# Row sums of a modulation vector on VectorE, a gate applied out of PSUM, and a bfloat16 exponential in a linear-attention and GEGLU block

## The chip, the cores and the metric

The kernel runs on 1 core of a Trainium2 chip. The metric is the device time of one execution in microseconds (us), as a median of several executions. Engines are named as in the profile: TensorE is PE (its weight loads PEld), VectorE is DVE, ScalarE is ACT, GpSimd is POOL and SyncE is SP. DMAs that an engine issues stand in its own queue, in order.

## The reference, cut to what matters

```python
mod = (silu(c) @ w_mod).reshape(...)          # 6 rows of 1024: sa, ca, ga, sb, cb, gb
h = layernorm(x) * (1 + ca) + sa
q, k, v = h @ wqkv                            # 32 heads of 32
phi = lambda t: where(t > 0, t + 1, exp(t)) + 1e-06
kv = einsum('bhsd,bhse->bhde', phi(k), v);  z = sum over s of phi(k)
o = (phi(q) @ kv) / (phi(q) . z + 1e-06)      # per head
x = x + ga * (o @ wo)
h = layernorm(x) * (1 + cb) + sb
x = x + gb * ((gelu(h @ w_gate) * (h @ w_up)) @ w_down)
```

Inputs are bfloat16: 2048 tokens of 1024 features, w_down has 3584 rows.

## The kernel before, in words

Sequence chunks are 128 tokens (16 of them), four chunks make a sequence group (sg). The work runs in stages along TensorE's queue:

- Start, 0 to 27 us: layer norm of the first chunks, and the modulation columns sa and ca by 128 narrow matmuls (L803).
- Feature-map stage, 27 to 127 us: blocks of 8 matmuls for k (L919) and q (L970), each into one PSUM bank. `phi` (L903) takes a bank out: ScalarE writes exp into a tile EB (L908), VectorE clamps EB in place (min 1, add 1e-6, L909), and VectorE adds max(bank, 0) and writes bfloat16 (L911). EB is float32, 128x512, five buffers.
- m tiles and W2, 127 to 205 us: 24 tiles of 16 matmuls (`m_tile`, L934; numbered 0 to 23 here) form phi(k)^T x per head group g. ScalarE copies a tile out (L939), SyncE issues a transposing DMA (`m_t`, tile mtb), `kv_prod` (L952) multiplies with the v weights, VectorE masks the result into KVT (L956, called kvt0 to kvt7), and `w2_pair` (L1235) multiplies KVT with two halves of wo. ScalarE copies the pair of banks out into W2 (L1237).
- From 192 us `wo_mm` (L1304) multiplies scaled phi(q) with W2, VectorE adds the residual (L1313, L1317), and the second layer norm and the GEGLU part (L1475, L1688) follow.

Four pieces of work are woven into the m tiles. The table `HOOK` in the code says after which tile each is recorded.

1. *The other modulation rows.* For half rows k = 0 to 7 (ga: 0 and 1; sb and cb: 2 to 5; gb: 6 and 7) VectorE accumulates silu(c) times w_mod, 8 steps of 128x512 each (macc, L855 and L858; for gb L833 and L835). The sum over the 128 partitions is done on TensorE: ScalarE rounds an accumulator to bfloat16 (mhi, L864, L842), VectorE takes the remainder (mlo, L868, L843), and `mod_rows` (L879) multiplies both with a column of ones, 8 matmuls of 32 columns by 256 or 512. ScalarE copies the bank (L886) and SyncE stores the row to DRAM (scr_row, L888). It is read back as a broadcast row (gab, L894, the gate ga on all partitions; gbb for gb) or as columns (sbT and cbT, L1252).
2. *The gate.* VectorE multiplies each of the 8 row blocks of wo with gab before W2 is formed (wofold, L1241).
3. *The denominators.* VectorE forms z32 (L1229). `den` (L1262) makes 32 matmuls for two sequence groups into bank 5; VectorE adds 1e-6 (dene, L1267), takes reciprocals (rden, L1268) in the buffer RDC and copies them to bfloat16 in the buffer RDH (rdenh, L1269). There is one RDC and one RDH. A store writes RDH to DRAM (scr_rd, L1271). den0 stands after tile 16 and its store directly behind it; den1 stands after tile 19.
4. *Scaling.* SyncE loads the factors back as broadcasts (rb, L1283) and VectorE scales phi(q) with them (pqs, L1296).

The order on VectorE, ScalarE and GpSimd from 27 us on isn't the recorded one: `Sched.reorder` sorts the operations by due times that it works out from a table of costs (`COST`) and from what depends on each. TensorE and SyncE keep the recorded order. Each engine waits on semaphores in its own order, so an operation that waits holds all behind it on that engine.

Of the kernel before, what the change touches and what calls it, by code (L numbers as in the profile page):

```python
# [7 lines left out]
ACTF = mybir.ActivationFunctionType  # L8
ALU = mybir.AluOpType

P = 128
# [178 lines left out]
class Sched:  # L190
# [41 lines left out]
    def dma(self, stream, fn, rd=(), wr=(), deps=(), note="", overwrite_ok=False):  # L232
# [6 lines left out]
        if prev is not None:  # L239
# [12 lines left out]
               "nm": (0.074, 0.085), "hmod": (0.25, 0.085), "macc": (0.66, 0.085), "mlo": (0.6, 0.085), "kvt": (0.21, 0.085), "z": (0.34, 0.085),  # L252
               "dene": (0.335, 0.085), "rden": (1.67, 0.085), "pqs": (0.62, 0.085), "wofold": (1.13, 0.085), "x": (1.14, 0.085), "ssum": (1.15, 0.085), "tsum": (1.15, 0.085), "padd": (0.62, 0.085), "yT": (0.62, 0.085)},
# [96 lines left out]
def bass_adaLN_cond__linear_attn_block__geglu_ffn__prompt_kernel(  # L350
# [18 lines left out]
    with ExitStack() as es:  # L369
# [48 lines left out]
        EB = [at(f"eb{i}", [P, 512], f32, EBO[i]) for i in range(5)]  # L418
# [4 lines left out]
        MROW = [at(f"mrow{i}", [P, 512], f32, OFF_ROW + i * 2048) for i in range(2)]  # L423
        MROW0 = at("mrowa", [P, 256], f32, XHO[2])
        WMG = [at(f"wmg{i}", [P, 4, 512], bf16, HBO[3] + i * 4096) for i in range(2)]
        MRG = at("mrg", [P, 256], f32, OFF_TMP + 4096)
        HLG = at("hlg", [P, 2, 2, 512], bf16, OFF_TMP)
        GAC = at("gacc", [P, 512], f32, OFF_TMP + 4096)
        ACC = [at(f"acc{i}", [P, 512], f32, OFF_ROW + i * 2048) for i in range(2)]
        HLO = OFF_WS + 16384  # L430
        HL = at("hl", [P, 4, 2, 512], bf16, HLO)
# [7 lines left out]
        for name, shape, dty, sz in [  # L439
            ("ident", [P, P], bf16, 256), ("bmask", [P, P], bf16, 256), ("bm32", [P, NG, NH], bf16, 512),   # L440
            ("z32", [P, NG, NH], bf16, 512), ("rdc", [P, SGW // 2], f32, 1024), ("rdh", [P, SGW // 2], bf16, 512),
            ("ones", [P, 32], bf16, 64), ("silf", [P, NDC], f32, 64),
# [14 lines left out]
        ONES, SILF, C8, CT, CHALF, THC, SILUT = (_small[k] for k in ("ones", "silf", "c8", "cT", "chalf", "thc", "siluT"))  # L457
# [78 lines left out]

        def r_hl(k, h0, h1):
            return [(HLO + (2 * (k % 4) + h0) * 1024, HLO + (2 * (k % 4) + h1) * 1024, "hl")]
# [131 lines left out]
        sch.op(V, lambda e: e.memset(ONES[:, :], 1.0), wr=r_sm("ones"))  # L670
# [155 lines left out]
        def r_hlg(j, h):  # L826
            return [(OFF_TMP + (2 * j + h) * 1024, OFF_TMP + (2 * j + h + 1) * 1024, "hlg")]

# [11 lines left out]
        def gb_hilo(j):  # L840
            acc, rng = GA_[j]
            sch.op(A, lambda e: e.activation(HLG[:, j, 0, :], acc[:, :], ACTF.Copy), rd=rng, wr=r_hlg(j, 0), note=f"mhi{6 + j}")  # L842
            sch.op(V, lambda e: e.tensor_tensor(HLG[:, j, 1, :], acc[:, :], HLG[:, j, 0, :], ALU.subtract), rd=rng + r_hlg(j, 0), wr=r_hlg(j, 1), note=f"mlo{6 + j}")  # L843

        o_gb = [None]

        def gb_rows():
            mod_rows(((0, 2, 5, lambda j, h: (HLG[:, j, h, :], r_hlg(j, h))),))
            o_gb[0] = mod_store(2, 5, MRG, [(OFF_TMP + 4096, OFF_TMP + 5120, "mrg")], 2)
# [12 lines left out]
        def mod_hi(k):  # L862
            rng = r_2k(OFF_ROW + k % 2 * 2048, f"acc{k % 2}")
            sch.op(A, lambda e: e.activation(HL[:, k % 4, 0, :], ACC[k % 2][:, :], ACTF.Copy), rd=rng, wr=r_hl(k, 0, 1), note=f"mhi{k}")  # L864

        def mod_lo(k):
            rng = r_2k(OFF_ROW + k % 2 * 2048, f"acc{k % 2}")
            sch.op(V, lambda e: e.tensor_tensor(HL[:, k % 4, 1, :], ACC[k % 2][:, :], HL[:, k % 4, 0, :], ALU.subtract),  # L868
                   rd=rng + r_hl(k, 0, 1), wr=r_hl(k, 1, 2), note=f"mlo{k}")

        def mod_rows(parts):
            for k0, n, bank, src in parts:
                o = None
                w = n * P
                for h in range(2):
                    for j in range(4):
                        ap, rng = src(k0 + j * n // 4, h)
                        ap = ap[:, j * w % 512:j * w % 512 + w]
                        o = sch.op(T, lambda e, h=h, j=j, ap=ap, bank=bank, w=w: e.matmul(  # L879
                            ps_all[32 * j:32 * (j + 1), bank * 512:bank * 512 + w], ONES[:, :], ap, start=(h == 0), stop=(h == 1)),  # L880
                            rd=rng + r_sm("ones"), pwr=(pr(bank) if h == j == 0 else ()), note=f"modr{k0}.{h}.{j}")
                pset_writer(bank, o)

        def mod_store(n, bank, dst, rng, row):
            w = n * P
            sch.op(A, lambda e: e.activation(dst[:, 0:w], ps_all[:, bank * 512:bank * 512 + w], ACTF.Copy),  # L886
                   prd=pr(bank), wr=rng, note=f"mrow{row}")
            return sch.dma(Q, lambda e: e.dma_start(scr_row[row, 0:n, :].rearrange("a (h b) -> (a h) b", b=w), dst[0:128:32, 0:w]), rd=rng, note=f"mrow{row}.st")  # L888

        def hl_src(k, h):  # L890
            return HL[:, k % 4, h, :], r_hl(k, h, h + 1)
# [214 lines left out]

        def wofold(*kcs):
            for kc in kcs:
                rg = r_wo(kc)
                sch.op(V, lambda e, kc=kc: e.tensor_tensor(WO[:, kc, :], WO[:, kc, :], GAB[:, :], ALU.mult),  # L1110
                       rd=rg + R_GAB, wr=rg, note=f"wofold {kc}")
# [978 lines left out]
```

## Time and profile before

| | |
|---|---|
| median of 3 runs | 784.59 us (783.88 to 785.09) |
| the profiled execution | 784.2 us, its span 782.4 us |
| TensorE's granted clock | 1.000 |
| VectorE, ScalarE busy in the span | 83%, 45% |
| 0 to 27 us, TensorE busy | 22.85 us |
| 27 to 127 us, TensorE / VectorE / ScalarE busy | 99.47 / 91.89 / 70.04 us |
| 127 to 205 us, TensorE / VectorE / ScalarE busy | 77.53 / 56.17 / 24.61 us |
| 205 to 260 us, TensorE / VectorE busy | 54.64 / 46.74 us |
| 260 to 600 us, TensorE / VectorE busy | 338.18 / 298.47 us |
| 600 to 782.4 us, TensorE / VectorE busy | 178.88 / 138.16 us |

The span goes from the first to the last instruction; the time of an execution is 1.8 us longer. A duration of one instruction in the groups includes its fill, so that the next one can start before it ends; where two follow each other, the distance of their starts is the cost. Line numbers are those of the kernel before; in the changed kernel the functions from `phi` on stand 27 to 41 lines higher.

### The profile page before, as it was taken

To read this page: it belongs to the slowest core of one execution; us is meant where nothing else is said; L and a number is where in the kernel's file an instruction comes from. 1 tells how busy PE (TensorE), PEld (TensorE's weight loads), DVE (VectorE), ACT (ScalarE), POOL (GpSimd) and SP (SyncE) were. 2 spreads that over 40 slices of the span, in tenths; PEclk is the share of its full clock that TensorE was granted. 3 is DMA by queue.
4 is the path that set the end of the run, shared out by engine and by line. 5 is a ranking of instruction groups with operands and counts; after the bars stand their busy time and mean duration, and the time that the engine had idled before them with its cause. 6 is when DMAs were issued, how large, how long until landed. Compare 5 with 4: busy or idle time off the path is not lost.

```text
span 782.4 us, 11038 instructions
## 1 busy us (share of the span) xinstructions
PE 771.6 (99%) x3812; PEld 501.1 (64%) x3875; DVE 646.0 (83%) x1089; ACT 353.0 (45%) x585; POOL 47.4 (6%) x126
## 2 busy tenths in 40 slices
PE   8999999999999999999999999999999999999998
PEld 4444445666445677767676777767676576677766
DVE  6699989993498978897999989898889897676777
ACT  2497743333474576776554444444544111111111
POOL 2031300000230011110000000000000000000000
PEclk9999999999999999999999999999999999999999
DMA  9889749836597068747445465646545445344341
GB/s 277 261 168 251 156 96 253 222 70 115 133 257 189 28 188 255 210 127 182 125 125 162 135 197 194 194 118 199 148 121 149 155 129 160 121 142 130 120 134 41
DMA packets 210543, 125.93 MB, mean 161 GB/s; under 512 B 70444, under 2 KB 200116, under 8 KB 210488
## 3 DMA queue, kind: packets, MB, share of 16 engines
q1 hardware_dynamic: 210328, 125.16, 58.4%
q8 instruction: 31, 0.51, 0.3%
q14 instruction: 24, 0.20, 0.1%
q10 hardware_dynamic: 160, 0.07, 0.0%
HBM read 88.35 MB, written 23.22 MB: 143 GB/s over the span
## 4 chain that ended last, share of the span: by engine, by line
PE 94%; DMA 2%; SPq 2%; issue 1%; DVE 0%; ACT 0%; DVEq 0%
PE ps_all L1475 45%; PE ps_all L1688 23%; PE ps_all L970 7%; PE ps_all L1304 7%; PE ps_all L934 6%; PE ps_all L919 6%; DMA mtb<-mb 1%; SPq L632 1%; DMA wmq<-in_w_mod_dram 1%; SPq L637 1%; PE ps_all L952 0%; PE ps_all L1235 0%; PE ps_all L1262 0%; SPq L626 0%; DVE xall L1317 0%
## 5 line engine op out<-in xcount | busy, mean ns | idle before, releaser
L1475 PE MATMUL ps_all<-ss,tp 128*128 128x512 f32 x896 | 214.7, 396 | 0.0
L1475 PEld LDWEIGHTS ps_all<-ss,tp 128*128 128x128 f32 x896 | 168.1, 188 | 38.2 <-DVE ps_all L1487 0.6
L1688 PE MATMUL ps_all<-bt,xs 128*128 128x512 f32 (+1 forms) x532 | 125.6, 393 | 0.1
L1688 PEld LDWEIGHTS ps_all<-bt,xs 128*128 128x128 f32 x532 | 98.9, 188 | 22.6 <-issue 0.5
L1487 DVE TENSOR_TENSOR ps_all<-ps_all,es 128x512 f32<-128x512 f32 x112 | 77.6, 696 | 38.4 <-PE ps_all L1475 35.8
L1492 ACT ACTIVATE ge<-ps_all 128x512 f32<-128x512 f32 x112 | 64.0, 597 | 89.1 <-DVE ps_all L1487 45.0
L1496 DVE TENSOR_TENSOR yr<-ge,ps_all 128x512 bf16<-128x512 f32 x112 | 74.0, 679 | 2.2 <-PE ps_all L1475 1.6
L1443 DVE TENSOR_TENSOR tp<-wt 128x512 fp32r<-128x512 bf16 x112 | 74.1, 683 | 1.1 <-DMA wt<-in_B_w_gate_dram 0.7
L1443 DVE TENSOR_TENSOR tp<-wt,tp 128x512 fp32r<-128x512 bf16 x112 | 74.0, 682 | 0.0
L970 PE MATMUL ps_all<-h1T,wq 128*128 128x512 bf16 x256 | 56.7, 379 | 0.0
L919 PE MATMUL ps_all<-wk,h1T 128*128 128x512 bf16 x239 | 55.3, 379 | 1.1 <-DMA wk<-in_A_wqkv_dram 0.5
L1304 PE MATMUL ps_all<-w,pq 128*128 128x512 bf16 x251 | 55.9, 379 | 0.4
L1688 PE MATMUL ps_all<-bx,yl 128*128 128x512 bf16 x225 | 55.2, 380 | 0.7
L1475 PE MATMUL ps_all<-ar,tp 128*128 128x512 f32 x224 | 55.3, 389 | 0.0
L908 ACT ACTIVATE eb<-ps_all 128x512 f32<-128x512 f32 x64 | 36.4, 593 | 37.5 <-PE ps_all L919 15.5
L1475 PE MATMUL ps_all<-h20a,wt 128*128 128x512 bf16 x210 | 48.0, 379 | 0.9
L1475 PE MATMUL ps_all<-h21a,wt 128*128 128x512 bf16 x210 | 47.8, 379 | 1.0
L1475 PEld LDWEIGHTS ps_all<-ar,tp 128*128 128x128 f32 x224 | 42.0, 188 | 8.7
L1484 ACT ACTIVATE es<-ps_all 128x512 f32<-128x512 f32 x56 | 33.4, 599 | 30.8 <-PE ps_all L1475 30.8
L1481 ACT ACTIVATE ps_all<-ps_all 128x512 f32<-128x512 f32 x56 | 32.6, 582 | 31.2 <-PE ps_all L1475 30.9
L970 PEld LDWEIGHTS ps_all<-h1T,wq 128*128 128x128 bf16 x256 | 25.0, 98 | 29.9
L1304 PEld LDWEIGHTS ps_all<-w,pq 128*128 128x128 bf16 x256 | 24.7, 98 | 30.3 <-issue 0.5
(152 smaller groups left out, 889.9 us busy)
## 6 DMA issues: line engine op xcount, KB each, us to landing
wt<-in_B_w_gate_dram SPq DMA_DIRECT2D x28, 512.0 KB, 4.0
wt<-in_B_w_up_dram SPq DMA_DIRECT2D x28, 512.0 KB, 5.4
scr_y<-yr SPq DMA_DIRECT2D x56, 256.0 KB, 4.8
yl<-scr_y SPq DMA_DIRECT2D x8, 896.0 KB, 4.7
yl<-scr_y SPq DMA_DIRECT2D x14, 448.0 KB, 4.4
wmst<-in_w_mod_dram SPq DMA_DIRECT2D x6, 1024.0 KB, 5.5
wmq<-in_w_mod_dram SPq DMA_DIRECT2D x8, 512.0 KB, 6.0
rb<-scr_rd SPq DMA_DIRECT2D x32, 128.0 KB, 2.9
```

Of the source, the lines that this page charges most:

```text
L908: sch.op(A, lambda e: e.activation(EB[i][:, :], PS(bank), ACTF.Exp), prd=pr(bank), wr=rng, note=f"{note}.exp")
L919: o = sch.op(T, lambda e, dc=dc: e.matmul(PS(bank), H1[sg][:, ci, dc, :], W_[:, dc, jg * 512:(jg + 1) * 512], start=(dc == 0), stop=(dc == ...
L934: o = sch.op(T, lambda e, c_=c_: e.matmul(PS(bank, 0, n), PK[c_][:, g * P:(g + 1) * P], xrow(c_, o_, o_ + n), start=(c_ == 0), stop=(c_ == ...
L970: o = sch.op(T, lambda e, dc=dc: e.matmul(PS(b), WQ[:, dc, qc * P:(qc + 1) * P], H1[sg][:, :, dc, :], start=(dc == 0), stop=(dc == NDC - 1 ...
L1304: last[half] = sch.op(T, lambda e, g=g, half=half: e.matmul(PS(b0 + half), PQ[sg][:, g, ci * P:(ci + 1) * P], W2[:, g, half * 512:(half + ...
L1443: sch.op(V, lambda e, t=t: e.tensor_tensor(TP[k][:, t, :, :], in0[:, t, :, :], in1[:, t, :, :], ALU.subtract), rd=r0[t:t + 1] + (r1[t:t + ...
L1475: o = sch.op(T, lambda e, l_=l_, r_=r_, dc=dc: e.matmul(PS(b), l_, r_, start=fresh and dc == 0, stop=dc == ND2 - 1, skip_group_check=True) ...
L1484: sch.op(A, lambda e: e.activation(ES[t][:, :], PS(be + t), ACTF.Copy), prd=pr(be + t), wr=r_2k(OFF_ES[t], f"es{t}"), note="escp")
L1487: sch.op(V, lambda e: e.tensor_tensor(PS(dst + t), PS(BB + t), ES[t][:, :], ALU.add), prd=pr(BB + t), rd=r_2k(OFF_ES[t], f"es{t}"), pwr=pr ...
L1492: sch.op(A, lambda e: e.activation(GE[i][:, :], PS(b), ACTF.Gelu_apprx_tanh), prd=pr(b), wr=r_2k(OFF_GE[i], f"ge{i}"), note="gelu")
L1496: sch.op(V, lambda e: e.tensor_tensor(YR[:, 2 * (v % 2) + l, h * SGW:(h + 1) * SGW], GE[i][:, :], PS(b + 1), ALU.mult), rd=r_2k(OFF_GE[i], ...
L1688: pend_ = sch.op(T, lambda e, l_=l_, r_=r_, i=i: e.matmul(PS(b, c0, c1), l_, r_, start=fresh and i == 0, stop=i == n - 1, skip_group_check ...
```

## The change

- EB is bfloat16 instead of float32; the exponential is written, and the clamp done, in bfloat16.
- The row sums no longer use TensorE and ScalarE. `part_sum` has VectorE transpose an accumulator in blocks of 32x32 (mtr) and sum over the 32 columns of each block (mred) into RDV. `mod_row` has VectorE copy the four quadrants of 32 partitions of a row's RDV side by side (qcp, four of 32x32), sum them (qred), transpose the 32x32 result (qtr), and SyncE stores it. There is one buffer each for QS, QR and QT; a later qtr waits for the store before it to have read QT. The rows sb and cb are now two rows with two stores (mrow1, mrow2), and sbT and cbT wait for both.
- wofold is gone. `w2_pair` has VectorE multiply the two banks with gab and write W2 (wtwo0 to wtwo7); ScalarE's copy is gone.
- den0 and den1 are recorded directly one after the other behind tile 16, den1 in bank 4 (kv_prod's bank), and den0's store is recorded behind tile 17 and before W2 pair 3. As den1's part is recorded before that store and RDH is one buffer, the store waits for den1's copy (rdenh1): the factors that go out for the first two sequence groups are den1's.
- kv1 is recorded after tile 10 instead of 9. After W2 pair 5, eight matmuls of the second output chunk stand between kv6 and kv7 instead of twelve, four more behind W2 pair 6, and six of the third chunk on each side of W2 pair 7.
- On SyncE the stores of sb and cb, sbT and cbT stand before kv4's transposing DMA as before; den0's store, which stood before that DMA, now stands behind it, before the first rb loads and kv5's transposing DMA.

```diff
-        EB = [at(f"eb{i}", [P, 512], f32, EBO[i]) for i in range(5)]
+        EB = [at(f"eb{i}", [P, 512], bf16, EBO[i]) for i in range(5)]
...
+        def part_sum(k):
+            acc, rng = GA_[k - 6] if k >= 6 else (ACC[k % 2], r_2k(OFF_ROW + k % 2 * 2048, f"acc{k % 2}"))
+            i = k % 2
+            rt = r_2k(TRO[i], f"tr{i}")
+            sch.op(V, lambda e: e.transpose(TR[i][:, :], acc[:, :]), rd=rng, wr=rt, note=f"mtr{k}")
+            sch.op(V, lambda e: e.tensor_reduce(RDV[:, k // 2, i * 16:i * 16 + 16], TR[i][:, :].rearrange("p (a b) -> p a b", b=32), mybir.AxisListType.X, ALU.add),
+                   rd=rt, wr=r_rd(k), note=f"mred{k}")
+
+        def mod_row(v, row, a0):
...
+            for q in range(HPG):
+                sch.op(V, lambda e, q=q: e.tensor_copy(QS[0:32, q, :], RDV[32 * q:32 * (q + 1), v, :]), ...)
+            sch.op(V, lambda e: e.tensor_reduce(QR[0:32, :], QS[0:32, :, :].rearrange("p q a -> p a q"), mybir.AxisListType.X, ALU.add), ...)
+            sch.op(V, lambda e: e.transpose(QT[0:32, :], QR[0:32, :]), rd=rr, wr=rt, note=f"qtr{v}")
+            return lambda: sch.dma(Q, ...)
...
-            sch.op(A, lambda e: e.activation(W2[:, g, :], ps_all[:, b0 * 512:(b0 + 2) * 512], ACTF.Copy),
-                   prd=pr(b0) + pr(b0 + 1), wr=r_w(OFF_WK, "w2", g), note=f"w2cp{g}")
+            sch.op(V, lambda e: e.tensor_tensor(W2[:, g, :], ps_all[:, b0 * 512:(b0 + 2) * 512], GAB[:, :], ALU.mult),
+                   prd=pr(b0) + pr(b0 + 1), rd=R_GAB, wr=r_w(OFF_WK, "w2", g), note=f"wtwo{g}")
...
-            mod_rows(((2, 4, 5, hl_src),))
-            o_r = mod_store(4, 5, MROW[1], r_2k(OFF_ROW + 2048, "mrow1"), 1)
+            o_r = [mod_row(v, 1, 2 * v - 2)() for v in (1, 2)]
...
-        HOOK = {0: "ga", 6: "kv0", 8: "w0", 9: "kv1", 11: "w1", 12: "kv2", 14: "w2 modp", 15: "kv3 z32", 16: "den0", 17: "w3", 18: "rb0.0",
-                19: "kv4 den1", 20: "w4 rb0.1", 21: "gbr", 22: "kv5", 23: ""}
+        HOOK = {0: "ga", 6: "kv0", 8: "w0", 10: "kv1", 11: "w1", 12: "kv2", 14: "w2 modp", 15: "kv3 z32", 16: "den0 den1", 17: "st0 w3", 18: "rb0.0",
+                19: "kv4", 20: "w4 rb0.1", 21: "gbr", 22: "kv5", 23: ""}
...
-                st[int(f[3:])] = den(int(f[3:]), 5)
-                if f == "den0":
-                    st[0]()
+                st[int(f[3:])] = den(int(f[3:]), 5 - int(f[3:]))
...
-            if 2 <= n <= 9:
-                wofold(n - 2)
...
-        wo_mm(1, 2, E6)
+        wo_mm(1, 2, E6[:4])
         kv_prod(7, 5)
...
+        wo_mm(1, 2, E6[4:])
+        wo_mm(2, 4, E6[:3])
         w2_pair(7)
-        wo_mm(2, 4, E6[4:])
+        wo_mm(2, 4, E6[3:])
```

More of the change, by code (lines that the diff above doesn't have):

```diff
@@ L422, in bass_adaLN_cond__linear_attn_block__geglu_ffn__prompt_kernel @@
         GBB = at("gbb", [P, D], f32, OFF_GBB)
[L423 to L424 removed]
         WMG = [at(f"wmg{i}", [P, 4, 512], bf16, HBO[3] + i * 4096) for i in range(2)]
[L426 to L427 removed]
         GAC = at("gacc", [P, 512], f32, OFF_TMP + 4096)
         ACC = [at(f"acc{i}", [P, 512], f32, OFF_ROW + i * 2048) for i in range(2)]
[L430 to L431 removed]
+        TRO = [OFF_WS + 16384, OFF_WS + 18432]
+        RDO, QSO, QRO, QTO = (OFF_WS + 20480 + i * 512 for i in range(4))
+        TR = [at(f"tr{i}", [P, 512], f32, TRO[i]) for i in range(2)]
+        RDV = at("rdv", [P, 4, NH], f32, RDO)
+        QS = at("qs", [P, HPG, NH], f32, QSO)
+        QR = at("qr", [P, NH], f32, QRO)
+        QT = at("qt", [P, NH], f32, QTO)
         KVT = at("kvt", [P, NG, P], bf16, OFF_KVT)
@@ L441, in bass_adaLN_cond__linear_attn_block__geglu_ffn__prompt_kernel @@
             ("z32", [P, NG, NH], bf16, 512), ("rdc", [P, SGW // 2], f32, 1024), ("rdh", [P, SGW // 2], bf16, 512),
-            ("ones", [P, 32], bf16, 64), ("silf", [P, NDC], f32, 64),
+            ("silf", [P, NDC], f32, 64),
             ("c8", [NDC, P], bf16, 256), ("cT", [P, NDC], f32, 64), ("chalf", [P, NDC], f32, 64),
@@ L871, in mod_rows @@
[L871 to L891, printed above, removed]
+        def r_rd(k, n=1):
+            return [(RDO + k * 64, RDO + (k + n) * 64, "rdv")]
@@ new lines, in mod_row @@
+        def mod_row(v, row, a0):
+            rq, rr, rt = ([(o_, o_ + w, n)] for o_, w, n in ((QSO, 512, "qs"), (QRO, 128, "qr"), (QTO, 128, "qt")))
+            for q in range(HPG):
+                sch.op(V, lambda e, q=q: e.tensor_copy(QS[0:32, q, :], RDV[32 * q:32 * (q + 1), v, :]), rd=r_rd(2 * v, 2), wr=[(QSO + q * 128, QSO + (q + 1) * 128, "qs")], note=f"qcp{v}.{q}")
+            sch.op(V, lambda e: e.tensor_reduce(QR[0:32, :], QS[0:32, :, :].rearrange("p q a -> p a q"), mybir.AxisListType.X, ALU.add), rd=rq, wr=rr, note=f"qred{v}")
+            sch.op(V, lambda e: e.transpose(QT[0:32, :], QR[0:32, :]), rd=rr, wr=rt, note=f"qtr{v}")
+            return lambda: sch.dma(Q, lambda e: e.dma_start(scr_row[row, a0:a0 + 2, :].rearrange("a (h i) -> (a h) i", i=32), QT[0:32, :]), rd=rt, note=f"mrow{v}.st")
```

49 lines of the change are left out of this document (10 added, 39 removed).

## The prediction, made before the changed kernel was run

> **What bounds the kernel now.** I read the page first, then the chain of waits, then the timelines of TensorE, VectorE and SyncE between 127 and 205 us. On the page the first row settles the bound: TensorE is busy 99% of the span, and its clock row is 9 throughout.
>
> ```profile
> PE 771.6 (99%) x3812; PEld 501.1 (64%) x3875; DVE 646.0 (83%) x1089; ACT 353.0 (45%) x585; POOL 47.4 (6%) x126
> ```
>
> So a gain must come out of TensorE's own queue, and a loss is a wait put into it. The table by stage says where there is anything to win: TensorE is busy 99.47 of 100 us in the feature-map stage (27 to 127) and 77.53 of 78 us in the stage of the m tiles and of W2 (127 to 205), which is where the change works. The chain of waits names what the change touches there (columns: start, length, what):
>
> ```profile
> 127.56 2.32 PE ps_all L934 x16
> 129.88 0.33 PE ps_all L879 x8
> ...
> 165.75 0.55 PE ps_all L879 x8
> ...
> 171.49 0.99 PE ps_all L1262 x32
> ...
> 180.53 0.99 PE ps_all L1262 x32
> ...
> 186.70 0.33 PE ps_all L879 x8
> ```
>
> An m tile takes 2.32 us; the three groups at L879 are the row sums by matmul, the two at L1262 are den. All five lie on the chain.
>
> **What TensorE loses.** I take start to start, since the pieces above leave out the switches between shapes. From the start of tile 0 to that of tile 1, 127.39 to 130.14, is 2.75, against 2.32 from tile 6 to the kv group behind it: the first row sum costs 0.43. The third (184.21 to 186.96) costs 0.43 as well. The second stands behind a W2 pair: 165.37 to 166.22 is 0.85, where the pair before it took 157.53 to 157.74, 0.21: 0.64. The den groups cost 1.08 (169.00 to 172.40 less 2.32) and 1.09 (179.91 to 181.45 less 0.45 for kv4); back to back they need one switch of 0.1 fewer, so 2.08: 0.09 saved. Two waits go too. kv1 starts 2.59 behind tile 9, 0.27 late, held by the transposed tile that landed at 152.16; the change puts it one tile later. kv4 is 0.10 late behind tile 19; whether that wait goes is the question below. Sum: 0.43+0.64+0.43+0.09+0.27+0.10 = **1.96 us**, in nominal places: kv4 due at 179.5, kv5 at 187.35, both worked out by moving the before starts by these terms (kv4 has den1's 0.99 ahead of it now).
>
> **What costs TensorE nothing.** The bfloat16 EB shortens at most the 64 clamps of L909 (419 ns, 0.34 start to start). Bounds: 0.02 (the bf16 scaling at L759 takes 397 ns for 512 elements) and 0.12 (0.22 for 128 elements, 8 of them in 1.87); fewer bytes move, so a loss is excluded. I take 0.1, since L759 reads two operands per partition beside its tile and L909 two constants: 6 us of VectorE in a stage in which TensorE has no gap to close, so 0. If the exponentials were dearer with the narrow output (ScalarE's bf16 copies at L864 take 628 ns, the exponential 593), 64 x 0.04 us would lie in ScalarE's 30 idle us of 100. The folding of WO (8 x 1.15 on VectorE) turns into 8 multiplications out of PSUM in place of ScalarE's W2 copies (8 x 1.02). The nearest row is the residual add at L1317: also PSUM by SBUF, 1024 wide, 1220 ns, 1.15 apart. The last of them has the least cover: W2[7] is wanted 8 matmuls (1.73 us) after its pair ends, and 0.26 from the end of a pair to the start of its copy (149.62 to 149.88) and 1.22 of work make 1.48. A multiplication over 1.47 us would delay the tail one for one.
>
> **Where it can be given back: VectorE's queue and, behind it, SyncE's.** VectorE works in order. The row sums leave ScalarE and TensorE and become, for each of eight half rows, a transpose and a sum on 128x512 f32, and for each of four rows six small operations. The trace has no 32x32 transpose and no reduction. Nearest row: the f32 subtraction at L868, 683 ns, 0.60 apart; the reciprocal (1748 ns for 256 elements, 3.5 us for 512) is the far end above, the 0.34 of L909 the end below. I take 0.60, since L868 streams as many elements of the same width. For the small ones the rows go from 60 ns (L643) to 208 (L994); I take 0.17.
>
> I walk VectorE's new order from 149.4 us, where wtwo0 waits for its pair (149.62 less 0.43, and 0.26 to wake). What stands before it is done by then: the gate row is loaded by about 140, as before. Up to rdenh1, the bfloat16 copy of den1's reciprocals, stand: 4 wtwo (4.60); 23 accumulations at 0.664 (15.27), 3 of them right behind the one they need (0.12 more each, from 4.68 for six at 149.75); 3 first products (1.18); 3 transposes and 2 sums (3.00); kvt1 to kvt3 (0.60); z32 (0.33); 6 small ones (1.0); two den rows, 0.33+1.66+0.20 each (4.38). Together 30.7, so rdenh1 is ready at **180.1**, and qtr2, which stands 8.2 ahead of it, at **171.9**.
>
> The Trainium skill ("VectorE: DVE Perf Modes", section "Two Vector instructions with no wait between them") says that a Vector instruction which reads from another quadrant of partitions than the one before starts only when all earlier ones are finished. That speaks against the four quadrant copies of a row; without it, at the 60 ns of L643 for each copy, the six would cost 0.6 rather than 1.0, and rdenh1 would come 0.4 earlier. No trace here shows such a copy.
>
> Now SyncE, also in order:
>
> ```profile
> 167.74 0.54 SPq L888 DMA_DIRECT2D scr_row<-mrow  x1
> 170.81 0.37 SPq L1252 DMA_DIRECT2D sbT<-scr_row  x1
> 171.23 0.58 SPq L1252 DMA_DIRECT2D cbT<-scr_row  x1
> 176.34 0.33 SPq L1271 DMA_DIRECT2D scr_rd<-rdh  x1
> 176.79 1.26 SPq L735 DMA_TRANSPOSE mtb<-mb  x1
> 178.14 2.02 SPq L1283 DMA_DIRECT2D rb<-scr_rd  x4
> 180.54 1.23 SPq L735 DMA_TRANSPOSE mtb<-mb  x1
> ```
>
> The second start is the wait for the row store to land: 3.07 us. (a) The second row store of the modulation pass now waits for qtr2, 172.0; sbT goes out at 175.1, cbT ends at 176.1, and only then kv4's transpose, whose tile is ready at about 175.2. Landing took 3.1 (the one issued at 180.54) to 4.4 us: 179.2 to 180.5, against 179.5. (b) den1 writes RDH before the first scr_rd store reads it, so that store waits for rdenh1 and carries den1's reciprocals: it goes out at 180.2, not 176.3. The rb loads follow 1.8 later (182.0), take 2.05, and kv5's transpose stands behind them: issued at 184.1, landed at 187.2 to 188.5, against 187.35. Each wait is 0 to 1.1; both hang on the same VectorE queue and kv4's wait moves kv5's due time, so I count one: 0.6, the middle. Behind kv5, pqs0.1 (rb0.1 lands about 189.5), wtwo5 and W2[5] (wanted 193.3, ready 192.5) still fit.
>
> **Sum.** -1.96+0.6 = **-1.4 us**. The profiled execution took 784.2 us (span 782.4 and 1.8 around it); the median of the three runs is 784.59, 0.4 above it, and I carry the difference over: **783.2**. From 205 us on everything follows TensorE and only shifts.
>
> **Rivals.**
> 1. No new wait: the transposes land in 3.1 us and VectorE keeps to 180.1. Then -1.96 and 782.6. For it: rb and transpose stood in the same order at 178.14 to 180.54, and that one landed in 3.1. Against it: cbT, 2.6 us in flight, now stands directly before kv4's transpose.
> 2. The change doesn't do what den back to back suggests: the first factors leave 3.9 us later, not earlier, and that takes the whole gain: landings at 4.4 and VectorE 0.9 late give 2.0, so 784.6.
> 3. The other side: transposes and sums cost twice the row of L868 or more. Five stand ahead of rdenh1, so at 1.2 us each it comes 3.0 later, kv4 and kv5 wait 3.6 in all, net +1.6: 786.2. It decides from about 1.2 us on; below that it only removes the gain. For it: no row shows them; at the reciprocal's pace (3.5 each) it would be 14.5 us and 797. Against it: every f32 row of 512 elements but the reciprocal lies at 0.34 to 0.66.
>
> **Numbers.** A measurement of this kernel can tell about 0.2% (1.6 us) from no change. Chances: the forecast 0.44, rival 1 0.30, rival 2 0.12, rival 3 0.14. Faster by over 0.2% means under 783.0: rival 1 and the near part (0.10) of the forecast, 0.40. Slower means over 786.2: rival 3 from its point on, 0.12, the rest of it within. Same: 0.48. Range 782.0 to 786.4: from rival 1 less the 0.6 that the runs before spread below their median, up to rival 3 at twice the row; its far end is left out with under 0.1.
>
> **What would show it.** Right: no matmuls of 32 columns but den's 64 in one piece; tile 0 to tile 1 in 2.32; kv4 and kv5 late by 0 to 1.1, released by the transposed tile; scr_rd's first store directly after the cast of den1. Wrong: the transpose rows above 0.8 us; TensorE waiting for z32 ahead of den, or for W2 in the tail; a feature-map stage shorter or longer than 100 us by over 0.3.

## The result and the profile after

The changed kernel takes 783.01 us (median of 12 executions, 781.97 to 784.56), the kernel before beside it 784.62 us (12 executions, 783.88 to 786.85). The ratio is 0.9976, 95% interval 0.9968 to 0.9984: 1.6 us faster by the medians, 1.9 by the ratio, which is not that of the medians. Measured once more with the last experiments, it took 782.67 us against 785.0, ratio 0.9971 (0.9961 to 0.9981). The profiled execution took 783.53 us, with a span of 780.7.

On the page of the changed kernel TensorE is as full as before, VectorE does the same total, and ScalarE does 13 us less (339.8 for 353.0):

```profile
PE 774.4 (99%) x3851; PEld 501.9 (64%) x3851; DVE 646.4 (83%) x1120; ACT 339.8 (44%) x566; POOL 44.7 (6%) x126
```

The equal total of VectorE hides two movements: 6.3 us less in the feature-map stage (85.60 for 91.89; the bfloat16 clamps alone take off 7.65, as an experiment below shows, and the row sum of ga puts some of it back) and 8.0 more in the stage of the m tiles (64.19 for 56.17, mostly the row sums; the multiplications by the gate take about the place of the foldings). The groups of VectorE from 27 to 205 us give the prices that no row of the kernel before showed (line, operation, shapes, count | busy us, mean ns | idle before, releaser):

```profile
L882 DVE TENSOR_SCALAR eb<-eb 128x512 bf16<-128x512 bf16 x64 | 17.1, 284 | 10.1 <-ACT eb L881 10.0
L1200 DVE TENSOR_TENSOR w<-ps_all,gab 128x1024 bf16<-128x1024 f32 x8 | 9.7, 1216 | 2.3 <-PE ps_all L1198 2.2
L855 DVE TENSOR_REDUCE rdv<-tr 128x16 f32<-128x512 f32 x8 | 5.0, 658 | 0.0
L854 DVE STREAM_TRANSPOSE tr<-acc 128x512 f32<-128x512 f32 x7 | 4.7, 688 | 0.0
L861 DVE COPY qs<-rdv 32x32 f32<-32x32 f32 x16 | 2.7, 169 | 0.4
```

The chain of waits between 127 and 205 us (start, length, what) now has no row sums. den is one piece of 64 matmuls, and the one wait to be seen stands ahead of the first kv group (L925):

```profile
143.69 0.26 issue
143.95 0.61 PE ps_all L925 x8
...
170.41 1.86 PE ps_all L1221 x64
...
179.78 0.62 PE ps_all L925 x8
```

"issue" means that the profile names no releaser. By start to start the wait is larger than the 0.26 shown, since the matmul ends are modelled: tile 0 starts at 127.28, seven tiles later the group is due at 143.53, and it starts at 143.95, 0.42 late. kv4 comes 0.16 late (179.78, due 179.62), kv1 and kv5 have no wait.

What kv0 waits for is its transposing DMA, and the timeline of SyncE shows why that is late:

```profile
128.06 0.45 SPq L864 DMA_DIRECT2D scr_row<-qt  x1
136.32 0.35 SPq L867 DMA_DIRECT2D gab<-scr_row  x1
136.73 0.43 SPq L819 DMA_DIRECT2D wmg<-in_w_mod_dram  x1
137.26 1.26 SPq L732 DMA_TRANSPOSE mtb<-mb  x1
...
175.57 0.38 SPq L1211 DMA_DIRECT2D sbT<-scr_row  x1
...
176.68 1.25 SPq L732 DMA_TRANSPOSE mtb<-mb  x1
180.52 0.34 SPq L1230 DMA_DIRECT2D scr_rd<-rdh  x1
182.15 1.83 SPq L1242 DMA_DIRECT2D rb<-scr_rd  x4
184.08 1.24 SPq L732 DMA_TRANSPOSE mtb<-mb  x1
```

In the kernel before, the same three transfers were:

```profile
130.78 0.65 SPq L888 DMA_DIRECT2D scr_row<-mrowa  x1
135.45 0.34 SPq L894 DMA_DIRECT2D gab<-scr_row  x1
...
136.37 1.27 SPq L735 DMA_TRANSPOSE mtb<-mb  x1
```

The row of the gate is stored 2.7 us earlier than before (128.06 for 130.78), but it is read back 0.9 later (136.32 for 135.45), because the store, issued right behind 2 MB of WO loads, lands only with them (the second load at 136.1, the store at 136.3). SyncE's waits say it in one line each, for the kernel before and the changed one (who waited <- for what: us in total, times, longest):

```profile
SPq L894 <- DMA scr_row<-mrowa: 3.9, 1, 3.9
```

```profile
SPq L867 <- DMA scr_row<-qt: 7.7, 1, 7.7
```

Everything recorded behind that load on SyncE is 0.9 late too, kv0's transposing DMA included (137.26 for 136.37). With no large load issued in the 5 us ahead of it such a store lands faster: the second store of the modulation rows ended on the queue at 172.85, and sbT followed at 175.57, 2.7 later. The Trainium skill, "DMA: Bandwidth & Descriptors", section "Queues, rings and completion order", says that each DMA engine takes descriptors in the order of its ring. The traces agree, with waits of 7.7 us behind 2 MB and 2.7 without, but they don't single that order out: in the last experiment a store that GpSimd issued, in another queue, still took 5.8 us to land while SyncE's transfers were in flight.

The gain is all in the m tiles. From the start of tile 0 to the first addition of the residual on VectorE (called the stage below), the kernel before takes 75.76 us (127.39 to 203.15) and the changed one 74.15 (127.28 to 201.43): 1.61 of the 1.7 us by which the spans differ.

### The profile page after: what moved, and what is told of

It reads as the page before. It is cut to its first block, busy times and chain, and to the rows that moved or that the text cites. A ratio compares the mean times of both kernels' runs of the same rounds, so it can differ in the third digit from the quotient of the medians.

```text
span 780.7 us, 11063 instructions
## 1 busy us (share of the span) xinstructions
PE 774.4 (99%) x3851; PEld 501.9 (64%) x3851; DVE 646.4 (83%) x1120; ACT 339.8 (44%) x566; POOL 44.7 (6%) x126
## 4 chain that ended last, share of the span: by engine, by line
PE 96%; SPq 2%; DMA 1%; issue 0%; DVE 0%
PE ps_all L1433 45%; PE ps_all L1646 23%; PE ps_all L907 7%; PE ps_all L1263 7%; PE ps_all L943 7%; PE ps_all L892 6%; DMA wmq<-in_w_mod_dram 1%; SPq L630 1%; SPq L635 1%; PE ps_all L925 1%; PE ps_all L1198 0%; PE ps_all L1221 0%; SPq L624 0%; PE ps_all L978 0%; PE ps_all L800 0%
## 5 line engine op out<-in xcount | busy, mean ns | idle before, releaser
L892 PE MATMUL ps_all<-wk,h1T 128*128 128x512 bf16 x248 | 56.9, 379 | 0.6 <-DVE h1T L756 0.6
L881 ACT ACTIVATE eb<-ps_all 128x512 bf16<-128x512 f32 x64 | 36.4, 596 | 40.9 <-PE ps_all L892 20.1
L1433 PE MATMUL ps_all<-h20a,wt 128*128 128x512 bf16 x224 | 51.0, 380 | 0.0
L1433 PE MATMUL ps_all<-h21a,wt 128*128 128x512 bf16 x224 | 50.9, 380 | 0.0
L1439 ACT ACTIVATE ps_all<-ps_all 128x512 f32<-128x512 f32 x56 | 32.6, 582 | 30.6 <-PE ps_all L1433 30.6
```

What stands on the lines that cost most here:

```text
L881: sch.op(A, lambda e: e.activation(EB[i][:, :], PS(bank), ACTF.Exp), prd=pr(bank), wr=rng, note=f"{note}.exp")
L892: o = sch.op(T, lambda e, dc=dc: e.matmul(PS(bank), H1[sg][:, ci, dc, :], W_[:, dc, jg * 512:(jg + 1) * 512], start=(dc == 0), stop=(dc == ...
L1433: o = sch.op(T, lambda e, l_=l_, r_=r_, dc=dc: e.matmul(PS(b), l_, r_, start=fresh and dc == 0, stop=dc == ND2 - 1, skip_group_check=True) ...
```

## The experiments

Twelve more runs followed, each timed beside the kernel before; one of them is the changed kernel again. The stage is read from the one profiled execution of each, and it orders them nearly as the ratios do:

| kernel | stage, us | ratio to before (95%) |
|---|---|---|
| before | 75.76 | 1 |
| changed | 74.15 | 0.9976 (0.9968 to 0.9984) |
| changed, again | 73.69 | 0.9971 (0.9961 to 0.9981) |
| changed, EB float32 | 73.63 | 0.9972 (0.9961 to 0.9982) |
| changed, den0's own factors | 74.23 | 0.9980 (0.9971 to 0.9989) |
| changed, small transfers by GpSimd | 74.68 | 0.9984 (0.9974 to 0.9995) |
| changed, loads moved | 75.09 | 0.9991 (0.9980 to 1.0001) |
| changed, both moves | 75.15 | 0.9990 (0.9981 to 0.9999) |
| changed, sums twice | 76.18 | 1.0001 (0.9993 to 1.0010) |
| all but the row sums | 75.10 | 0.9989 (0.9980 to 0.9998) |
| before, EB bfloat16 | 76.01 | 0.9993 (0.9984 to 1.0002) |
| row sums and gate | 76.74 | 1.0017 (1.0006 to 1.0028) |
| row sums only | 78.11 | 1.0022 (1.0012 to 1.0032) |
| row sums and order | 78.88 | 1.0025 (1.0012 to 1.0038) |

The shortest stage, 73.63, has no wait of TensorE: seven tiles from tile 0 to kv0 (16.26), and each group at its place behind. It serves below as the stage without waits.

### Row sums only

The functions of the row sums as in the changed kernel; all else as before (EB float32, wofold and ScalarE's W2 copy, the old HOOK and tail). Against the changed kernel:

```diff
-        HOOK = {..., 10: "kv1", ..., 16: "den0 den1", 17: "st0 w3", 18: "rb0.0", 19: "kv4", ...}
+        HOOK = {..., 9: "kv1", ..., 16: "den0", 17: "w3", 18: "rb0.0", 19: "kv4 den1", ...}
-            sch.op(V, lambda e: e.tensor_tensor(W2[:, g, :], ps_all[...], GAB[:, :], ALU.mult), ...)
+            sch.op(A, lambda e: e.activation(W2[:, g, :], ps_all[...], ACTF.Copy), ...)
+            if 2 <= n <= 9:
+                wofold(n - 2)
```

> The kernel before with one part of the change: the row sums by VectorE. The gate is still folded into WO, EB is float32, den0 and den1 stand where they stood. Theory A (TensorE's queue sets the time; its row-sum matmuls are worth 0.43 + 0.64 + 0.43 = 1.50 us, and the early row store costs 0.4 at kv0 because SyncE waits for its landing behind the WO loads): tile 0 to tile 1 in 2.32, the first kv group again late by about 0.4, together -1.1 us against the kernel before. Rival B (the late kv0 comes from the other parts, the clamps or the new order): the first kv group is on time and the whole 1.5 comes out. Rival C (VectorE's own work is what was exchanged, no gain): within 0.3 of the kernel before.

Measured: 786.48 us against 784.66, ratio 1.0022 (1.0012 to 1.0032): 1.8 us slower. None of the three expected it. The row-sum matmuls are gone (tile 0 to tile 1 in 2.32), but TensorE's timeline has three waits in their place:

```profile
144.43 0.61 PE L925 MATMUL ps_all<-mtb,wv 128*128 128x128 bf16 x8 [0.82 <-issue]
...
154.12 0.62 PE L925 MATMUL ps_all<-mtb,wv 128*128 128x128 bf16 x8 [1.69 <-DMA mtb<-mb]
...
182.50 0.62 PE L925 MATMUL ps_all<-mtb,wv 128*128 128x128 bf16 x8 [1.25 <-DMA mtb<-mb]
```

Start to start they are 0.99 (kv0), 1.84 (kv1) and 1.43 (kv4), where the kernel before had 0, 0.27 and 0.10. So -1.50 for the matmuls and +3.9 for waits give +2.4, as the stage shows (78.11 less 75.76 is 2.35). The chain names the two roots:

```profile
143.74 10.34 DMA mtb<-mb
...
178.63 0.21 DVE rdh L1231
...
178.91 0.34 SPq L1233
...
179.35 3.10 DMA mtb<-mb
```

kv1's transposing DMA is 10.34 us in flight behind two 1 MB loads of w_mod; kv4's stands on SyncE behind the first store of the factors, and that store waits for the copy of den0's reciprocals (rdh) in VectorE's queue, 2.5 us later than before (178.56 for 176.03), with eight foldings, started 2.2 late (142.30 for 140.06), ahead of it.

### All but the row sums

The kernel before with bfloat16 EB, the gate out of PSUM, the new HOOK and tail; the row sums by TensorE and ScalarE as before. The first store carries den1's factors here too.

> The whole change except the row sums, which stay with ScalarE and TensorE: bfloat16 EB, the gate applied out of PSUM, den0 and den1 back to back, kv1 one tile later, and the first store of the factors behind den1, so that it carries den1's factors as it does in the changed kernel. Theory A: den back to back gives 0.1 to 0.2, kv1's wait 0.27, kv0 stays on time as before: -0.3 to -0.5 us against the kernel before, far less than the changed kernel's. Rival B (taking the folding and the copies off VectorE and ScalarE is what brings the gain): -1 us or more. Rival C (the multiplication out of PSUM is on the path): slower by up to 0.5.

Measured: 783.59 us, ratio 0.9989 (0.9980 to 0.9998), between theory A and rival B; the stage is 0.66 shorter than before and shows no wait of TensorE at all. 0.37 of that are the waits of kv1 and kv4, and 0.2 is den in one piece (1.96 with its switches for 1.08 and 1.09 apart). Its stage is longer than the shortest one by 75.10 - 73.63 = 1.47: that is what the row-sum matmuls cost when nothing else is late, 1.50 predicted.

The two kernels together say that the parts aren't additive: row sums alone +2.35 in the stage, the rest alone -0.66, both -1.6 to -2.1. The next two ask which of the rest is needed.

### Row sums and gate

The kernel of row sums only, with the multiplication out of PSUM in place of wofold and ScalarE's copy.

> The kernel before with the row sums by VectorE and the gate applied out of PSUM, all else (float32 EB, kv1 at tile 9, den0 and den1 apart, the order of the tail) as before. It is the first kernel of the experiments, which lost 1.8 us, with the folding taken off VectorE. Theory A (that kernel lost through three waits with two causes: kv0 and kv1 by transfers that land late behind SyncE's wait for the row store, kv4 by VectorE's queue, in which eight foldings stand ahead of den0's factors): the kv4 wait of 1.4 goes, the kv1 wait of about 1.9 stays, 785.0 us, 0.3 above the kernel before. Rival B (everything hangs on VectorE's queue): the kv1 wait goes as well, 783.2. Rival C (the foldings have nothing to do with it): all three waits stay, 786.4.

Measured: 786.3 us, ratio 1.0017 (1.0006 to 1.0028); the stage falls from 78.11 to 76.74. Theory A was half wrong: two waits stay, and by the time alone rival C (786.4) is nearest, although kv0's wait is gone.

```profile
152.80 0.62 PE L925 MATMUL ps_all<-mtb,wv 128*128 128x128 bf16 x8 [1.29 <-DMA mtb<-mb]
...
181.04 0.62 PE L925 MATMUL ps_all<-mtb,wv 128*128 128x128 bf16 x8 [1.12 <-DMA mtb<-mb]
```

kv0 is on time in this execution. By start to start kv1 is 1.45 late: 0.27 as before, 0.43 because it is due sooner by the first row sum's matmuls, and 0.7 because its tile, issued as early as before, is 10.34 in flight and not 9.66. kv4 is 1.3 late although the foldings are gone, and not because TensorE gets there earlier (kv1's wait has used that up): one of W2's multiplications (1.16 us, at 175.40) now stands between den0's reciprocals and their copy, which comes at 176.47 for 176.03, and the transposing DMA behind the store of the factors goes out at 177.28 for 176.79 and takes 0.6 longer on the queue. So the gate alone doesn't mend the order.

### Row sums and order

The kernel of row sums only, with the new HOOK and tail (the first store carries den1's factors); the gate folded into WO by VectorE.

> The kernel before with the row sums by VectorE and the new order (kv1 one tile later, den0 and den1 back to back, the store behind den1, which then carries den1's factors, and the changed tail), float32 EB and the gate folded into WO as before. Theory A: the kv1 wait is covered by the extra tile, the kv4 transpose no longer stands behind den0's store, but VectorE has eight foldings ahead of den1's factors, which come at about 182 in place of 180; the kv5 group waits some 1.5 us: about 784.3 us, between the kernel before and the changed one. Rival B (the order alone mends it): no wait at kv5, 782.7. Rival C (VectorE's queue holds the whole stage): as slow as with the row sums alone, 786.4.

Measured: 787.4 us, ratio 1.0025 (1.0012 to 1.0038), the slowest of all, with the longest stage (78.88). Rival C came nearest. kv0, kv1 and, but for 0.3, kv4 are on time, as the order should have it; kv7 is 0.5 late. But VectorE now bounds the stage, at a place that no theory named:

```profile
142.94 5.71 DVE L1204 TENSOR_TENSOR wo<-wo,gab 128x1024 bf16<-128x1024 bf16 x5
148.59 0.27 DVE L929 TENSOR_TENSOR kvt<-ps_all,bmask 128x128 bf16<-128x128 f32 x1
...
158.89 0.28 DVE L929 TENSOR_TENSOR kvt<-ps_all,bmask 128x128 bf16<-128x128 f32 x1
```

```profile
159.46 0.61 PE L1198 MATMUL ps_all<-wo,kvt 128*128 128x512 bf16 x1 [2.53 <-DVE kvt L929]
159.86 2.20 PE L907 MATMUL ps_all<-xrow,pk 128*128 128x341 bf16 x7
161.85 1.98 PE L907 MATMUL ps_all<-xall,pk 128*128 128x341 bf16 x9
```

In the kernel before, the foldings started 2.9 earlier:

```profile
140.06 5.77 DVE L1241 TENSOR_TENSOR wo<-wo,gab 128x1024 bf16<-128x1024 bf16 x5 [0.81 <-DMA gab<-scr_row]
```

Here the row sums of the next row stand ahead of them. The foldings and the accumulations leave VectorE no gap from 142.94 on, and kvt1, behind them, comes at 158.89; in the changed kernel it came at 155.66. W2 pair 0 waits 0.29 for kvt0 and W2 pair 1 2.53 for kvt1. This kernel differs from the changed one with float32 EB (below) by the gate alone, and its stage is 5.25 longer. Not all of that is waiting: the tile behind W2 pair 1, the last two lines of TensorE above, takes 3.81 from start to start and not 2.32. From 159.5 to 162.9 TensorE's granted clock was 0.50 in this execution, which costs 1.5 us, and the waits make up the other 3.8. Six of this kernel's twelve executions have a mean clock of 0.998, as the profiled one has, so the half clock is a part of its median too; whether the wait just ahead brings it about was not tested. VectorE's work for the gate is the same size in both, 9.3 us of foldings and 9.7 of multiplications; but the foldings all stand ahead of kvt1, and of the multiplications one does, and four of the eight stand behind den1's factors.

### EB in float32, and EB in bfloat16 alone

One line each, in the changed kernel as shown and in the kernel before the other way round:

```diff
-        EB = [at(f"eb{i}", [P, 512], bf16, EBO[i]) for i in range(5)]
+        EB = [at(f"eb{i}", [P, 512], f32, EBO[i]) for i in range(5)]
```

> The changed kernel with EB in float32 again (clamps, additions and the rest of the change as they are). Theory A (in the feature-map stage TensorE is busy 99 of 100 us, VectorE has room): no difference from the changed kernel, within 0.3 us, although VectorE is busy about 8 us longer in that stage. Rival B (the bfloat16 EB pays something, for example by bringing the last tiles of the stage out earlier): 0.3 to 1 us slower than the changed kernel. Rival C (the narrow exponential costs time somewhere): faster by as much.

> The kernel before with EB in bfloat16 and nothing else. Theory A: no difference from the kernel before, within 0.3 us; VectorE's busy time falls by about 8 us, all in the feature-map stage. Rival B (the narrow EB is part of the gain): 0.3 us or more faster. Rival C: 0.3 us or more slower, through ScalarE.

Measured: with float32 782.31 us, ratio 0.9972 (0.9961 to 0.9982), where the changed kernel has 0.9976 and 0.9971; with bfloat16 alone 784.46 us, 0.9993 (0.9984 to 1.0002). Neither can be told from no difference: theory A. VectorE is 7.9 us less busy with bfloat16 alone (638.1 for 646.0), 7.65 of them in the feature-map stage or 0.12 per clamp, and TensorE doesn't wait there in either kernel.

### Sums twice

```diff
-            sch.op(V, lambda e: e.transpose(TR[i][:, :], acc[:, :]), ...)
-            sch.op(V, lambda e: e.tensor_reduce(RDV[...], TR[i]..., ALU.add), ...)
+            for _ in range(2):
+                sch.op(V, lambda e: e.transpose(TR[i][:, :], acc[:, :]), ...)
+            for _ in range(2):
+                sch.op(V, lambda e: e.tensor_reduce(RDV[...], TR[i]..., ALU.add), ...)
```

> The changed kernel with every 128x512 transpose and every block sum of the row sums done twice, with the same result: 16 more VectorE instructions of about 0.6 us each, of which five stand ahead of the factors of den1. Theory A (VectorE's queue reaches TensorE only through SyncE's chain: row store, sbT and cbT, the kv4 transpose; factors, rb, the kv5 transpose): the last cast of the factors comes about 3 us later and the kv4 and kv5 groups together wait 2.5 to 3 us longer, so +2.5 to +3 us against the changed kernel; this is also the price of rival 3 of the prediction. Rival B (that chain has slack): within 0.5 us of the changed kernel. Rival C (VectorE works back to back through the whole stage and bounds it): more than +5 us.

Measured: 784.73 us, ratio 1.0001 (0.9993 to 1.0010): some 2 us slower than the changed kernel and level with the one before. The stage is 2.0 to 2.5 longer than the two of the changed kernel. The main place is one of the two expected ones, and the price is smaller than 2.5 to 3:

```profile
190.55 0.62 PE L927 MATMUL ps_all<-mtb,wv 128*128 128x128 bf16 x8 [1.52 <-DMA mtb<-mb]
```

That is kv5, 1.7 late by start to start, held by SyncE's chain behind den1's factors, stored at 182.51 for 180.52; kv4 is on time within 0.1, and kv3 and den are 0.3 and 0.2 late. Counted from W2's first multiplication the store is only 1.1 later, not 3, since four of the added instructions stand ahead of it (2.4 us) and the planner (`Sched.reorder`, which sorts VectorE's operations) moved one transpose and one accumulation of gb (1.3), which nobody waits for there, behind the factors.

### Loads behind the transposing DMAs

```diff
-            row_load(GAB, R_GAB, 0, 0, "gab", mod_row(0, 0, 0)())
+            o_ga[0] = mod_row(0, 0, 0)()
...
             if k == 2:
                 m_t(g)
+            if n == 2:
+                row_load(GAB, R_GAB, 0, 0, "gab", o_ga[0])
+            if n == 17:
+                sc_load()
```

> The changed kernel with two groups of loads moved on SyncE: the load of the gate row is issued behind the transposing DMA of the first kv group, and the loads of sbT and cbT behind that of the fifth (kv4). Theory A (the transposing DMAs are late only because SyncE waits ahead of them for the landing of a row store): the waits of 0.42 at kv0 and 0.16 at kv4 go, kv5 stays on time, -0.5 us against the changed kernel. Rival B (the transposing DMA of kv0 is late because of the 2 MB of WO loads in flight, wherever it stands): kv0 stays late by 0.4, no difference. Rival C (the gate row, now later, makes the first products of W2 late and takes it back): W2's first multiplication starts later than 149.8 us, and the total is the same or slower.

Measured: 783.96 us, ratio 0.9991 (0.9980 to 1.0001), 1 us slower than the changed kernel. Theory A was right about the two waits, kv0 and kv4 are on time (16.26 from tile 0; 5.08 from W2 pair 3), and wrong about what follows. SyncE still waits for the row store, and now the loads of w_mod stand behind that wait. VectorE's timeline shows it at the first accumulation of half row 4, where the changed kernel waited 2.02:

```profile
148.95 0.49 DVE L840 TENSOR_SCALAR acc<-wmst,silf 128x512 f32<-128x512 bf16 x1 [4.00 <-DMA wmst<-in_w_mod_dram]
```

```profile
157.63 0.61 PE L1200 MATMUL ps_all<-wo,kvt 128*128 128x512 bf16 x2 [0.52 <-DVE kvt L929]
...
189.05 0.61 PE L925 MATMUL ps_all<-mtb,wv 128*128 128x128 bf16 x8 [0.52 <-DMA mtb<-mb]
```

Two accumulations move behind W2's first multiplication, and kvt1 comes at 157.29 for 155.66; W2 pair 1 waits for it, and kv5 for the chain behind den1's factors (stored at 181.74 for 180.52). Rival C had the outcome but not the place: the first multiplication starts at 149.83, as in the changed kernel (149.78).

### den0's own factors

```diff
-        HOOK = {..., 16: "den0 den1", 17: "st0 w3", ...}
+        HOOK = {..., 16: "den0 st0 den1", 17: "w3", ...}
```

> The changed kernel with the first store of the factors recorded ahead of den1, so that it carries den0's own factors; den1's group and its reciprocals stand where they stand. Theory A (the store's place decides nothing, since rb and the kv5 transpose have room): no difference from the changed kernel, within 0.3 us; the store goes out about 2 us earlier, and the second cast waits for its landing. Rival B (the late store is what holds the kv5 transpose): kv5 starts earlier and the total is 0.2 to 0.6 faster. Rival C (the wait of the second cast for the store, some 2 us at the head of VectorE's queue, holds the accumulations and the W2 products behind it): 0.3 to 1 us slower.

Measured: 783.33 us, ratio 0.9980 (0.9971 to 0.9989); no difference that can be told from the changed kernel. In the profile the store's place does decide something, though not at kv5: the store goes out at 176.90, and kv4's transposing DMA, which it is ahead of again, at 177.35. That is 2.58 behind the start of W2 pair 3, where it was 2.14 in the changed kernel.

```profile
180.50 0.62 PE L925 MATMUL ps_all<-mtb,wv 128*128 128x128 bf16 x8 [0.48 <-DMA mtb<-mb]
```

By start to start kv4 is 0.65 late here and was 0.16 in the changed kernel: the store's place behind the DMA buys 0.5 in the profile. In the medians the difference can't be seen.

### Both moves

The edits of the last two kernels together.

> The changed kernel with both moves of the two kernels named before: loads of the rows behind the transposing DMAs, and den0's factors stored ahead of den1. Theory A: the gains of the two add, -0.5 us against the changed kernel, 782.4 to 782.5 where the changed kernel takes 783.0. Rival B (they meet on SyncE: the early store's landing and the loads of sbT and cbT now stand in one queue ahead of rb): kv5 late by 0.3 to 0.8, and the gain is lost.

Measured: 783.9 us, ratio 0.9990 (0.9981 to 0.9999). The losses of both kernels are there: W2 pair 1 waits 0.52 for kvt1, kv4 0.59 for its transposing DMA. The gain is lost, as rival B has it, but in neither theory's place: kv5, where rival B expected it, is on time.

### The changed kernel again, and the small transfers on GpSimd's queue

```diff
-            return lambda: sch.dma(Q, ...)
+            return lambda: sch.dma(G, ...)
```

The same edit stands at the loads of gab, sbT and cbT and at den0's store, which is recorded ahead of den1.

> The changed kernel once more, unaltered, beside the others on the same chip. Theory A (its waits at kv0 and kv4 hang on how the loads of WO happen to drain, 0.4 us of one execution): 782.6 to 783.1 us, and in this profile the kv0 wait may be smaller or gone. Rival B (the waits are fixed): 0.42 and 0.16 again.

> The changed kernel with the small row transfers on GpSimd's queue, which is idle in this stage: the store of the gate row and its load, the two stores of the modulation rows with the loads of sbT and cbT, and den0's store, which is recorded ahead of den1 and so carries den0's own factors. SyncE then waits for none of them ahead of a transposing DMA. Theory A (kv0 and kv4 are late only through SyncE's waits): tile 0 to the first addition of x1 in about 73.6 us with no wait of TensorE, as in the best profile so far, 782.3 us, 0.6 below the changed kernel. Rival B (the transfers land late because the queues are full, whoever issues them): kv0 late by 0.4 as before, the same as the changed kernel. Rival C (a transfer issued by GpSimd takes longer to land, and the gate row or the factors come too late): slower than the changed kernel.

The changed kernel again: 782.67 us, ratio 0.9971 (0.9961 to 0.9981), as theory A has it. Its profile has no wait at kv0 (16.25 from tile 0) nor at kv4. SyncE waited 6.8 us for the row store and kv0's transposing DMA went out at 136.42, 9.04 us behind tile 0 (127.38), where it was 9.98 in the first profile. Over the profiles of the kernels with VectorE's row sums this distance tells whether kv0 waits: 7.7 to 9.66 in eight of them, no wait; 9.98, 10.38 and 10.64 in the other three, and waits of 0.42, 0.38 and 0.99.

With GpSimd's queue: 783.73 us, ratio 0.9984 (0.9974 to 0.9995), no better than the changed kernel. kv0 and kv4 are on time, and kv0's transposing DMA goes out at 134.61, since SyncE has no row store to wait for: the waits were SyncE's. But the gate comes too late. Timelines of GpSimd, VectorE and TensorE in this kernel:

```profile
136.69 0.83 POOL L864 DMA_DIRECT2D scr_row<-qt  x1 [48.40 <-DVE eb L882]
142.75 0.59 POOL L867 DMA_DIRECT2D gab<-scr_row  x1 [5.24 <-DMA scr_row<-qt]
```

```profile
155.94 1.22 DVE L1200 TENSOR_TENSOR w<-ps_all,gab 128x1024 bf16<-128x1024 f32 x1
```

```profile
157.44 0.38 PE L1198 MATMUL ps_all<-wo,kvt 128*128 128x512 bf16 x1 [1.15 <-DVE w L1200]
```

Here the planner set VectorE's row sum of ga later (the transposed row is ready at 136.18; in the changed kernel its store was out at 128.06) and W2's first multiplication at 155.94 in place of 149.78, so that W2 pair 1 waits for its banks. Most of that is VectorE's order: gab took 8.1 us to land (5.1 in the changed kernel, issued by SyncE ahead of other loads), but it was there at 150.83, 1.1 us after the time of the multiplication in the changed kernel and 5.1 before it starts here. The kernel was not tried with VectorE's order held, so what GpSimd's queue costs by itself stays open. No kernel of this study beats the changed one by more than the measurement can tell.

## Why the prediction was right, point by point

The forecast was 783.2, and 783.01 and 782.67 were measured.

- **The matmuls (-1.50).** Right: 1.47 between two kernels that have no wait. den in one piece costs 1.96 with its switches in place of the 2.08 taken, so it saves 0.2 and not 0.09. With kv1's and kv4's waits the sum was to be 1.96; the stage without waits is shorter than that of the kernel before by 75.76 - 73.63 = 2.13.
- **VectorE's walk.** Its length is right to 0.1: from W2's first multiplication to the end of den1's copy it takes 30.6 (149.78 to 180.38) and 30.7 were taken. It starts 0.4 late, behind kv0's wait, so that the copy is done 0.3 late (180.1 forecast) and qtr2 0.5 late (172.4 for 171.9). Transposes are 0.62 and sums 0.59 apart (0.60 taken), multiplications 1.14 (1.15). The six small operations take 1.2 and not 1.0: the four copies are 0.20 apart. The prediction cited a rule of the Trainium skill for them ("VectorE: DVE Perf Modes", section "Two Vector instructions with no wait between them"), by which a copy that reads from another quadrant of partitions than the instruction before starts only when all earlier ones are finished. The trace agrees: the second to fourth copies of a row each start 0.03 us after the instruction before has ended, while the first copies of three rows, from the same quadrant as the instruction before, start 0.07 to 0.08 before it ends.
- **SyncE's chain.** Right to 0.5: sbT at 175.57 (175.1), the store of the factors at 180.52 (180.2), rb at 182.15 (182.0), kv5's transposing DMA at 184.08 (184.1).
- **The wait of 0.6 counted at kv4 or kv5: this is the term that was mis-sized.** It measured 0.16 in one profile (kv4) and 0.12 in the other (kv5, 187.27, due 187.15). kv4's tile landed 3.1 and kv5's 3.4 to 3.5 us after its issue, the early part of the 3.1 to 4.4 taken. Instead 0.42 stood at kv0 in the first profile and nothing in the second. That 0.42 and 0.16 make nearly the 0.6 counted is luck, since the larger one lies where the prediction looked for no wait. The prediction had taken the gate row to be loaded by about 140, "as before", and looked no further: it followed the early row store into VectorE's queue only, not into SyncE's, where the wait for its landing holds a transposing DMA. By the mechanism rival 1 (782.6, no new wait) is nearer than the forecast.
- **bfloat16 EB: 0.** Right within the measurement. 0.12 us per clamp was at the upper bound.
- **Rival 3** priced the transposes at twice the row at +1.6 over the kernel before. Done twice they gave 1.0001: the place was right (kv5), the price about 1.5 us too high, because work that nobody waits for moved behind the factors.
- **What the prediction did not see** is larger than any of these. It gave each part its own term and added. The row sums by VectorE, worth 1.50, lose 1.8 us when they come alone. They pay only because the same change moves kv1 one tile back (2.32 of cover for a wait of 1.45 to 1.84), puts kv4's transposing DMA ahead of the store of the factors, and takes the foldings from ahead of kvt1. The order was tried as a whole, and of its parts the place of the store alone; kv1's move was not run by itself. The sum came out right since it was made for the whole change; the same terms would have been wrong for each of the three parts with the row sums that were run.

## What to carry to other kernels

Work taken from the bounding engine makes every arrival behind it due sooner, and the engine and the queue that take the work over deliver later: list the arrivals that were just in time (here kv1's tile, 0.27 late already, and kv4's, 0.10), and move their consumers or their issue in the same change. An earlier store brings nothing if it is queued behind large loads and the queue that issued it waits for its landing; ask what stands behind that wait. And work of equal size is not equal in place: 9.3 us of foldings ahead of the stage's second W2 pair cost 3.8 us of waits (and 1.5 more at half the clock) against 9.7 us of multiplications spread over the stage.

## What the runs showed of the hardware

- A transposing DMA took 3.0 us from issue to landing at the best, and 9.7 to 11.6 us behind loads of w_mod, two of them of 1 MB (the longest of each of the fourteen profiles).
- A 4 KB row store, issued right behind two 1 MB loads, took 7.0 to 8.9 us to land (ten profiles), and in other places of the stage 1.3 to 3.4 us when SyncE issued it; between two executions of the changed kernel SyncE's wait for it differed by 0.9 (7.7 and 6.8), enough to make kv0 late in one and not in the other.
- The 32x32 block transpose of 128x512 float32 on VectorE takes 688 ns, and the next instruction can follow after 0.62; the sum over the blocks' columns 658 ns and 0.59; four 32x32 copies from four quadrants 169 ns each and 0.20 apart, each after the end of the one before.
- The clamp of 128x512 takes 284 ns in bfloat16 and 419 in float32; the exponential 596 and 593.
- TensorE's granted clock was 0.50 for 3.4 us right behind a wait of 2.53 us in the profile of the row sums with the new order, and a tile of 16 matmuls took 3.81 us in place of 2.32. Behind the wait of 1.69 us in the kernel of row sums only, the next tiles took 2.32.
